# Attention feeding a top-1 mixture of experts on one core: pooled values as 128 and 16 tokens, zero matmuls ahead of the last steps, another order of the attention step

## The chip, the cores and the metric

The kernel runs on 1 core of one Trainium2 chip. The metric is the device time of an execution in microseconds (us). Before the change it was 737.2 us, the median of three runs (732.1 to 743.44).

## The reference

The input has 8 batches of 8 heads with 576 tokens of 64 values. Each head's output is the sum of two attentions: one over the tokens at a distance under 4, and one over sequences pooled by 4 (144 tokens), whose output is repeated four times. The heads side by side give 4608 tokens of 512 values, which pass through the one of eight experts whose embedding lies nearest.

```python
q_d = q.reshape(B, H, Sd, factor, D).mean(axis=3)
k_d = k.reshape(B, H, Sd, factor, D).mean(axis=3)
v_d = v.reshape(B, H, Sd, factor, D).mean(axis=3)
out_up = np.repeat(sm_attn(q_d, k_d, v_d), factor, axis=2)
...
mask = np.abs(pos[:, None] - pos[None, :]) < factor
scores = np.where(mask, scale * np.matmul(q, k.transpose(0, 1, 3, 2)), -1000000000.0)
...
return (out_up + np.matmul(attn, v)).astype(np.float32)
```

```python
logits = xn @ en.T / tau
expert_idx = np.argmax(logits, axis=1)
...
h = np.maximum(x[mask] @ w1[e], 0.0)
out[mask] = gate_w[mask, None] * (h @ w2[e])
```

## The kernel before

**Attention.** A unit of work is one batch and two heads; there are 32 units. `attention()` runs a loop over `i` from -2 to 32, and each pass is one step of a pipeline that has four units in flight. What a pass does is a list of names in `ORDER` (L44). A name with digits is a call of `op_<name>` with these digits as arguments, and `LEAD` says for which unit: the transposes and pooled sums of q and k (`qkT`, `kc`, `pk`, `pq`, `kdT`, `qd`) for unit i+2, the scores and their softmax (`mask scores mx sub expa scd md expd asum add rec an adn`) and the pooled values (`pv`, `vd`) for i+1, the weighted sums (`wT aT wdT adT vald od val xT`) for i, and turning the result into token rows with its logits (`rowsT lastT xr lgt lastrow ls`) for i-1. Nothing reorders these calls: every engine executes its part of them in the order in which they are written, so the table is the order of each engine's queue.

On TensorE (PE), `qkT` (L372) transposes 96 tokens at a time; `mask` (L417) and `scores` (L425) give the local scores, 36 matmuls of 32 queries by 38 keys; `wT` (L483) transposes the local weights `an` into 70 x 128 pieces; `scd` (L445) gives the pooled scores and `wdT` (L495) transposes the pooled weights `ad` in two pieces along the 144 pooled tokens; `vald` (L508) multiplies these with the pooled values `vd`, in two parts that add up in PSUM; `val` (L521) multiplies `aT` with the windows of v (`vw`); `rowsT` and `lastT` (L532) transpose the sum `xT` into rows, and `lgt` (L558) gives the logits. ScalarE (ACT) evicts most of these (`kc` L379, `aT` L490, `adT` L501) and takes the exponentials. VectorE (DVE) does the maxima, sums and scalings (`an` L472, `ad` in `adn` L477, `md` L450, `rec` L467). GpSimd (POOL) makes the pooled sums: `pq` and `pk` L388, `kdT` L399, `qd` L404 and, of the values, `pv` L408 and `vd` L413. All PSUM results rotate through eight banks.

**Loads.** All loads are issued on SP's queue. The k and q of two units (L339) are issued after the last `qkT` of an odd unit, the windows of v (`load_w`, eight transfers, L356 and L362) after its last `val`, and the pooled values (`load_v`, L347) of unit u+3 after `vd` of unit u. A pooled value load reads 4 consecutive tokens into one partition: 72 partitions, twice, with both heads and 256 values.

**What else is in a step.** `Y0` and `Y1` are places at which `attention()` yields to the caller, which may put a slot of expert work there. In the middle of attention that is the first expert's weights: squares (L832) and the splitting of a weight into two half-precision parts, by ACT (L856) and DVE (L857). Near the end, at the pairs in `EARLY`, it is the preparation of the first token lists: `parts` on DVE (L654, L658), 30 small matmuls (L666), `ids` (L670 to L673), and the gathers of rows (L1110). `mid` and `tail` run pieces of `place()`, which once in four units stores a batch's rows (`xd`), finds each token's expert and counts them (L610, L612). `warm_up(n)` issues n matmuls of 128x512 whose result nobody reads.

**Experts.** From about 287 us on, 41 groups of 128 tokens go through two layers of matmuls with split weights (L1213 to L1251).

Of the kernel before, what the change touches and what calls it, by code (L numbers as in the profile page):

```python
# [8 lines left out]
F32 = mybir.dt.float32  # L9
# [10 lines left out]
B, H, S, D = 8, 8, 576, 64  # L20
N, DM, E, FF = B * S, H * D, 8, 1024
NHP = H // 2
SD = S // 4
G, QB = S // 64, 32
WK, WV = QB + 6, 64 + 6
CD = SD // 2
CP = S // 6
TB = 128
NTB = -(-S // TB)
# [12 lines left out]
FIRST = 3  # L42
EARLY = ((8, 1), (9, 1), (10, 1), (11, 1), (27, 0), (27, 1), (28, 0), (29, 0), (29, 1), (30, 0), (30, 1), (31, 0), (31, 1), (32, 1))
ORDER = """  # L44
qkT11 qkT01 qkT10 qkT00 kc11 kc10 mask scores kc01 mx wT1 pq wT0 sub qd1 kc00 mid scd md Y0 qd0 wdT1 pk
wdT0 aT1 aT0 tail share wT2 adT1 kdT pv0 adT0 pv1 expa lastT expd0 lgt asum vald expd2 rowsT expd1 aT2
lastrow od val0 ls add rec Y1 val1 vd an0 an1 xr xT0 xT1 adn
""".split()
FIRST_ORDER = """
mask scores qkT00 qkT01 qkT10 qkT11 kc00 kc10 kc01 kc11 mx sub expa pk pq kdT qd0 qd1 scd md expd0 expd1  # L50
# [12 lines left out]
class Kern:  # L63
# [128 lines left out]
    def attention(self, ctx):  # L192

        nc = self.nc
# [3 lines left out]
        z = self.pool(ctx, "zeroed", 1)  # L198
        self.kq, self.an, self.qdbd, self.vw, self.xT, self.sums = [], [], [], [], [], []
        for i in range(2):  # L200
            self.kq.append(z.tile([128, 2, S + 6], F32, name=f"kq{i}"))
            self.qdbd.append(z.tile([128, 3, 2, 48], F32, name=f"qdbd{i}"))
            self.xT.append(z.tile([128, NTB * TB], F32, name=f"xT{i}"))
            self.an.append(z.tile([128, G, WV], F32, name=f"an{i}"))
            self.sums.append(z.tile([128, G + 3], F32, name=f"sums{i}"))
            self.vw.append(z.tile([WV, G, 4, D], F32, name=f"vw{i}"))
        self.lg = z.tile([TB, NTB, E + 1], F32, name="lg")
        self.oh = self.cp.tile([TB, B, NTB + 1, E], BF16, name="oh")
        units = [(b, hp) for b in range(B) for hp in range(NHP)]
        n = len(units)  # L210
        st, half = {}, {}

        def load(j):
            if j < n // 2:
                half[j] = self.load(j // 2, j % 2)

        pair = {}

        def load_v(u):
            if u < n:  # L220
                pair[u] = self.load_v(*units[u])

        def load_w(j):
            if j < n // 2:
# [9 lines left out]
        for i in range(2):  # L234
            nc.vector.memset(self.kq[i][:, :, :3], 0.0)
            nc.vector.memset(self.kq[i][:, :, S + 3:], 0.0)
            nc.vector.memset(self.vw[i][:32, 0], 0.0)
            nc.vector.memset(self.vw[i][64:, G - 1], 0.0)
            for h in range(2):
                nc.vector.memset(self.qdbd[i][h * D:(h + 1) * D, :, 1 - h], 0.0)  # L240
                nc.vector.memset(self.an[i][h * 64:(h + 1) * 64, :, QB * (1 - h) + 6 * (1 - h):][:, :, :QB], 0.0)
            nc.vector.memset(self.xT[i][:, S:], 0.0)
            nc.vector.memset(self.sums[i], 1.0)
        next(crows)
        load(1)
        load_v(0)
        load_w(0)
        load_v(1)
        lead = {name: k for k, names in LEAD.items() for name in names.split()}

        def table(order):
            ops = []
            for op in order:
                name = op.rstrip("012")
                ops.append((name, [int(x) for x in op[len(name):]]))
            return ops, {name: j for j, (name, _) in enumerate(ops)}

        tail, mid, xr = [], [], {}
        for i in range(-2, n + 1):
            if i == n - 2:  # L260
                self.warm_up(2)
            ops, final = table(FIRST_ORDER if i < NFIRST else ORDER)
            weights = max(final["wT"], final["wdT"])
            for j, (name, args) in enumerate(ops):
# [10 lines left out]
                else:  # L275
                    u = i + lead[name]
# [5 lines left out]
                    s = st[u]  # L282
# [31 lines left out]
            if i >= 1 and units[i - 1][1] == NHP - 1:  # L314
                for f in tail:
                    f()
                b = units[i - 1][0]
                tail = self.place(b, xr[b]["xr"], xr[b]["ls"], mid)
# [20 lines left out]
                    nc.sync.dma_start(out=s[nm][:, :, c], in_=src[b, 4 * hf + c].rearrange("(p m) d -> p m d", m=6))  # L339
        return s  # L340

    def load_v(self, b, hp):
        nc, ld = self.nc, self.ld
        h = slice(2 * hp, 2 * hp + 2)
        vr = ld.tile([CD, 2, 2, 4 * D], F32, name="ld_v", bufs=3)
        for c in range(2):
            nc.sync.dma_start(out=vr[:, c], in_=self.v[b, h, c * S // 2:(c + 1) * S // 2].rearrange(  # L347
                "h (i r) d -> i h (r d)", r=4))
        return vr

    def load_w(self, b, hf, vw):
# [52 lines left out]
        s["g"].tensor_tensor(out=self.qdbd[s["u"] % 2][hs, :, h, :], in0=q2[:, :, :, 0], in1=q2[:, :, :, 1], op=ALU.add)  # L404

    def op_pv(self, s, c, v):
        s["v"], vr = v, v[:, c]
        self.nc.gpsimd.tensor_tensor(out=vr[:, :, 0:2 * D], in0=vr[:, :, 0:2 * D], in1=vr[:, :, 2 * D:], op=ALU.add)  # L408

    def op_vd(self, s):  # L410
        v, vd = s["v"], self.wk.tile([CD, 2, 2, D], F32, name="vd")
        s["vd"] = vd
        self.nc.gpsimd.tensor_tensor(out=vd, in0=v[:, :, :, 0:D], in1=v[:, :, :, D:2 * D], op=ALU.add)  # L413

# [75 lines left out]
        self.nc.scalar.activation(out=dst, in_=s["wT", c], func=AF.Copy)  # L490

    def op_wdT(self, s, c):
        pt = s["wdT", c] = self.bank()[:CD, :288].rearrange("p (c q) -> p c q", c=3)
        for cc in range(3):
            self.nc.tensor.transpose(out=pt[:, cc], in_=s["ad"][:, cc, c * CD:(c + 1) * CD],  # L495
                                     identity=self.ident[:96, :96])

    def op_adT(self, s, c):
        if "adT" not in s:
            s["adT"] = self.wk.tile([CD, 2, 2, 3, 48], F32, name="adT", bufs=1)  # L500
        self.nc.scalar.activation(out=s["adT"][:, c].rearrange("p h c j -> p c h j"),  # L501
                                  in_=s["wdT", c].rearrange("p c (h j) -> p c h j", h=2), func=AF.Copy)

    def op_vald(self, s):
        pd = s["vald"] = self.shared[:, TB:TB + SD]
        for c in range(2):
            for h in range(2):
                self.nc.tensor.matmul(out=pd[h * D:(h + 1) * D], lhsT=s["vd"][:, c, h, :],  # L508
                                      rhs=s["adT"][:, c, h].rearrange("p c j -> p (c j)"),
                                      start=(c == 0), stop=(c == 1))  # L510

    def op_od(self, s):
# [884 lines left out]
```

## Time and profile before

| | before |
|---|---|
| runs | 732.1, 737.2, 743.44 us |
| the profiled execution | 739.52 us, span 737.7 us, mean granted clock 0.972 |
| PE busy | 705.5 us (96%) |
| DVE, ACT, POOL busy | 470.4, 464.9, 444.0 us |
| moved by the core's own queue of loads (q1) | 118.15 MB, 74.8% of 16 engines |

The span is what the trace covers; the profiled execution's own time is 1.8 us longer. "Busy" counts the time in which an engine has an instruction running; PE's ends are modelled, so a busy PE need not be one at its peak. A matmul in the timeline is given as out<-in by the program's names, then the stationary tile (rows*columns) and the moving tile. In brackets stands the idle time ahead of an instruction and what ended it.

### The profile page before, as it was taken

How to read it: one execution, taken by the hardware profiler on the slowest of the kernel's cores; microseconds unless marked ns; L12 is line 12 of the kernel's file. 1: busy time of each engine (PE TensorE's matmuls, PEld its weight loads, DVE VectorE, ACT ScalarE, POOL GpSimd, SP SyncE). 2: the span in 40 equal slices, each digit the busy share in tenths (PEclk: the TensorE clock that was granted, in tenths of full speed). 3: DMA queues.
4: the chain of work that ended last, by engine and by line, in shares of the span. 5: the costliest groups of instructions: out<-in, count | busy, mean ns of one | idle time of the engine just before them, and what ended most of it. 6: DMA issues, size and time to landing. Idle time of an engine off the chain costs nothing. (4 is left out here: it accounts for less than half of the span.)

```text
span 737.7 us, 22025 instructions
## 1 busy us (share of the span) xinstructions
PE 705.5 (96%) x7463; PEld 422.3 (57%) x7463; DVE 470.4 (64%) x1415; ACT 464.9 (63%) x1063; POOL 444.0 (60%) x854
## 2 busy tenths in 40 slices
PE   8999999999999989999999999999999999999992
PEld 5787787878778765454444444444444444444440
DVE  6778789868998775686646566565553455366320
ACT  4777778678787563556666577675665556557420
POOL 4865778766868875366656564646556655664420
PEclk9999899999999887999999999999999999999996
DMA  9899899999888974869988979988997599769830
GB/s 159 168 215 191 209 195 227 215 200 212 164 203 177 207 234 115 194 146 235 218 171 220 241 200 192 225 241 201 225 213 166 116 223 222 151 176 204 168 74 19
DMA packets 283861, 138.92 MB, mean 188 GB/s; under 512 B 250930, under 2 KB 260146, under 8 KB 283712
## 3 DMA queue, kind: packets, MB, share of 16 engines
q1 hardware_dynamic: 276992, 118.15, 74.8%
q0 software_dynamic: 6560, 19.03, 8.1%
q8 instruction: 61, 1.00, 0.6%
q14 instruction: 88, 0.72, 0.3%
q10 hardware_dynamic: 160, 0.02, 0.0%
HBM read 213.05 MB, written 20.33 MB: 316 GB/s over the span
## 5 line engine op out<-in xcount | busy, mean ns | idle before, releaser
L1249 PE MATMUL bank<-w2h,hT 128*128 128x512 f16 x328 | 124.3, 379 | 0.9 <-ACTq L994 0.9
L1214 PE MATMUL bank<-w1l,xT 128*128 128x512 f16 x328 | 124.5, 380 | 0.1
L1215 PE MATMUL bank<-w1h,xT 128*128 128x512 f16 x328 | 124.5, 380 | 0.0
L1213 PE MATMUL bank<-w1h,xT 128*128 128x512 f16 x328 | 124.4, 379 | 0.0
L1251 PE MATMUL bank<-w2h,hT 128*128 128x512 f16 x328 | 124.3, 379 | 0.0
L1250 PE MATMUL bank<-w2l,hT 128*128 128x512 f16 x328 | 124.3, 379 | 0.0
L1110 POOL DMA_INDIRECT xg<-xd,ids x41 | 46.0, 1121 | 79.4 <-POOLq L994 33.6
L1226 ACT ACTIVATE h<-bank 128x512 f16<-128x512 f32 x82 | 48.3, 589 | 56.5 <-PE bank L1215 51.0
L1262 POOL DMA_INDIRECT out_dram<-o,ids x41 | 46.6, 1136 | 47.3 <-ACTq L994 16.6
L379 ACT ACTIVATE kq<-bank 128x288 f32<-128x288 f32 x128 | 48.9, 473 | 34.6 <-PE bank L372 33.5
L832 ACT ACTIVATE junk<-st 128x1024 bf16<-128x1024 f32 (+1 forms) x30 | 67.5, 2251 | 4.1 <-DMA xd<-xr 2.1
L1258 ACT ACTIVATE o<-bank,gt 128x512 f32<-128x512 f32 x41 | 27.8, 677 | 62.0 <-issue 16.3
L408 POOL TENSOR_TENSOR ld_v<-ld_v 72x256 f32<-72x256 f32 x64 | 50.2, 801 | 21.3 <-DMA ld_v<-in_v_dram 20.2
L388 POOL TENSOR_TENSOR pool_kq<-kq 128x288 f32<-128x288 f32 x62 | 44.9, 725 | 30.0 <-ACT kq L379 30.0
L81 POOL TENSOR_SCALAR nw_t<-nw_y,nw_a 128x1 f32<-128x1 f32 x123 | 53.1, 432 | 12.4
L1230 DVE SCALAR_TENSOR_TENSOR h<-bank,h 128x512 f16<-128x512 f32 x82 | 56.3, 687 | 2.7 <-ACTq L1003 2.2
L857 DVE SCALAR_TENSOR_TENSOR w2l<-st,wscl,w2h 128x1024 f16<-128x1024 f32 x32 | 39.6, 1281 | 28.2 <-ACT w2h L856 28.2
L490 ACT ACTIVATE aT<-bank 70x384 f32<-70x384 f32 x96 | 43.9, 490 | 20.7 <-PE bank L483 20.6
L1213 PEld LDWEIGHTS <-xT 128*128 128x128 f16 x328 | 35.2, 107 | 34.0
L1250 PEld LDWEIGHTS <-hT 128*128 128x128 f16 x328 | 32.1, 98 | 39.4 <-issue 1.2
L1215 PEld LDWEIGHTS <-xT 128*128 128x128 f16 x328 | 32.0, 98 | 39.2 <-issue 0.7
L1251 PEld LDWEIGHTS <-hT 128*128 128x128 f16 x328 | 32.1, 98 | 38.7
(220 smaller groups left out, 1559.2 us busy)
## 6 DMA issues: line engine op xcount, KB each, us to landing
st<-in_moe_w_dram SPq DMA_DIRECT2D x148, 1024.0 KB
ld_k<-in_k_dram SPq DMA_DIRECT2D x64, 144.0 KB
ld_q<-in_q_dram SPq DMA_DIRECT2D x64, 144.0 KB
ld_v<-in_v_dram SPq DMA_DIRECT2D x64, 144.0 KB
xd<-xr SPq DMA_DIRECT2D x8, 1040.0 KB
st<-in_moe_w_dram SPq DMA_DIRECT2D x16, 512.0 KB
vw<-in_v_dram SPq DMA_DIRECT2D x64, 122.5 KB
vw<-in_v_dram SPq DMA_DIRECT2D x32, 64.0 KB
```

What stands on the lines that cost most here:

```text
L81: g.tensor_scalar(out=t, in0=y, scalar1=y, scalar2=a, op0=ALU.mult, op1=ALU.mult)
L379: self.nc.scalar.activation(out=dst, in_=s["qk", r, w].rearrange("p (m i) -> p i m", m=3), func=AF.Copy, scale=(KSC, QSC)[w])
L408: self.nc.gpsimd.tensor_tensor(out=vr[:, :, 0:2 * D], in0=vr[:, :, 0:2 * D], in1=vr[:, :, 2 * D:], op=ALU.add)
L832: self.nc.scalar.activation(out=junk, in_=src, func=AF.Square, accum_out=acc)
L1213: nc.tensor.matmul(out=ps, lhsT=xT[:, 0, k], rhs=self.w1h[:, k, ns], start=(k == 0), stop=False)
L1214: nc.tensor.matmul(out=ps, lhsT=xT[:, 0, k], rhs=self.w1l[:, k, ns], start=False, stop=False)
L1215: nc.tensor.matmul(out=ps, lhsT=xT[:, 1, k], rhs=self.w1h[:, k, ns], start=False, stop=(k == self.KC - 1))
L1226: self.nc.scalar.activation(out=h2[:, 0], in_=ps, func=AF.Relu)
L1230: self.nc.vector.scalar_tensor_tensor(out=h2[:, 1], in0=ps, scalar=0.0, in1=h2[:, 0], op0=ALU.max, op1=ALU.subtract)
L1249: nc.tensor.matmul(out=ps, lhsT=hh, rhs=self.w2h[:, j, :], start=(j == 0), stop=False)
L1250: nc.tensor.matmul(out=ps, lhsT=hh, rhs=self.w2l[:, j, :], start=False, stop=False)
L1251: nc.tensor.matmul(out=ps, lhsT=hl, rhs=self.w2h[:, j, :], start=False, stop=(j == self.FC - 1))
```

## The change

Three parts. `CD`, the number of pooled tokens in each of the two pieces, goes from 72 and 72 to 128 and 16; with it the pooled value loads, `pv`, `wdT`, `adT` and the two parts of `vald` have 128 and 16 rows (or columns). The tiles for the loads are no longer taken from a rotating pool but are three fixed ones, whose second halves POOL sets to zero once at the start, since `vd` adds all 128 partitions of both halves. `warm_up` is called ahead of the last three passes (2, 2 and 6 matmuls) instead of once (2). And `ORDER` is another table.

```diff
-CD = SD // 2
+CD = (128, SD - 128)
...
 ORDER = """
-qkT11 qkT01 qkT10 qkT00 kc11 kc10 mask scores kc01 mx wT1 pq wT0 sub qd1 kc00 mid scd md Y0 qd0 wdT1 pk
...
+qkT10 qkT01 qkT00 mask qkT11 kc01 kc00 kc11 scores mx wT2 kc10 aT2 sub wT1 wT0 aT1 pq qd0 scd aT0 wdT1 qd1
...
+        self.vr = [z.tile([128, 2, 2, 4 * D], F32, name=f"ld_v{i}") for i in range(3)]
...
-                pair[u] = self.load_v(*units[u])
+                pair[u] = self.load_v(*units[u], self.vr[u % 3])
...
+        for vr in self.vr:
+            nc.gpsimd.memset(vr[:, 1], 0.0)
...
-            if i == n - 2:
-                self.warm_up(2)
+            if i >= n - 2:
+                self.warm_up((2, 2, 6)[i - n + 2])
...
-    def load_v(self, b, hp):
-        nc, ld = self.nc, self.ld
-        h = slice(2 * hp, 2 * hp + 2)
-        vr = ld.tile([CD, 2, 2, 4 * D], F32, name="ld_v", bufs=3)
-        for c in range(2):
-            nc.sync.dma_start(out=vr[:, c], in_=self.v[b, h, c * S // 2:(c + 1) * S // 2].rearrange(
-                "h (i r) d -> i h (r d)", r=4))
+    def load_v(self, b, hp, vr):
+        h, t0 = slice(2 * hp, 2 * hp + 2), 0
+        for c, n in enumerate(CD):
+            self.nc.sync.dma_start(out=vr[:n, c], in_=self.v[b, h, t0:t0 + 4 * n].rearrange("h (i r) d -> i h (r d)", r=4))
+            t0 += 4 * n
         return vr
...
-        s["v"], vr = v, v[:, c]
+        s["v"], vr = v, v[:CD[c], c]
...
-        v, vd = s["v"], self.wk.tile([CD, 2, 2, D], F32, name="vd")
+        v, vd = s["v"], self.wk.tile([128, 2, 2, D], F32, name="vd")
...
-        pt = s["wdT", c] = self.bank()[:CD, :288].rearrange("p (c q) -> p c q", c=3)
+        pt = s["wdT", c] = self.bank()[:CD[c], :288].rearrange("p (c q) -> p c q", c=3)
         for cc in range(3):
-            self.nc.tensor.transpose(out=pt[:, cc], in_=s["ad"][:, cc, c * CD:(c + 1) * CD],
+            self.nc.tensor.transpose(out=pt[:, cc], in_=s["ad"][:, cc, c * CD[0]:c * CD[0] + CD[c]],
                                      identity=self.ident[:96, :96])
...
-                self.nc.tensor.matmul(out=pd[h * D:(h + 1) * D], lhsT=s["vd"][:, c, h, :],
-                                      rhs=s["adT"][:, c, h].rearrange("p c j -> p (c j)"),
+                self.nc.tensor.matmul(out=pd[h * D:(h + 1) * D], lhsT=s["vd"][:CD[c], c, h, :],
+                                      rhs=s["adT"][:CD[c], c, h].rearrange("p c j -> p (c j)"),
                                       start=(c == 0), stop=(c == 1))
```

What the new table moves, engine by engine. The queue of PE over the second half of a steady step, from the local scores to the weighted sums, before (the names are those of the tiles, the sizes rows and columns of the operands as the program writes them):

```order
L425 MATMUL bank<-kq_109 32x38 x36
L483 MATMUL bank<-ident,an_106 70x128 x6
L445 MATMUL bank<-kdT,qdbd_110 96x144 x3
L495 MATMUL bank<-ident,ad 72x96 x6
L483 MATMUL bank<-ident,an_106 70x128 x3
L532 MATMUL bank<-ident,xT_111 128x128
L558 MATMUL bank<-xT_111,enT 32x192 x4
L508 MATMUL bank<-adT,vd 64x144 x4
L532 MATMUL bank<-ident,xT_111 128x128 x4
L521 MATMUL bank<-aT,vw_114 64x64 x18
```

and with the change:

```order
L426 MATMUL bank<-kq_109 32x38 x36
L484 MATMUL bank<-ident,an_106 70x128 x9
L446 MATMUL bank<-kdT,qdbd_110 96x144 x3
L496 MATMUL bank<-ident,ad 16x96 x3
L496 MATMUL bank<-ident,ad 128x96 x3
L533 MATMUL bank<-ident,xT_111 128x128 x4
L559 MATMUL bank<-xT_111,enT 32x192 x4
L533 MATMUL bank<-ident,xT_111 128x128
L509 MATMUL bank<-adT,vd 64x144 x4
L522 MATMUL bank<-aT,vw_108 64x64 x18
```

All nine transposes of `an` now stand ahead of the pooled scores, the pooled weights are transposed as 16 and 128, and four of the five row transposes stand ahead of the logits and of `vald`. Ahead of these rows, `mask` has moved between the third and the fourth of the `qkT`.

The queue of DVE in a step in which a weight is split (L857, with the change L858), before:

```order
L472 TENSOR_TENSOR an_112<-a,sums_113 64x9x38 x2
L526 TENSOR_TENSOR xT_105<-bank,od 128x320
L526 TENSOR_TENSOR xT_105<-bank,od 128x256
L477 TENSOR_TENSOR ad<-ad,sums_113 96x432
L432 TENSOR_REDUCE mx<-bank 128x9
L436 TENSOR_TENSOR a<-bank,mx 128x342
L450 TENSOR_REDUCE md<-bank 96x3
L857 SCALAR_TENSOR_TENSOR w2l<-st_483,wscl,w2h 128x1024
```

and with the change:

```order
L473 TENSOR_TENSOR an_106<-a,sums_107 64x9x38 x2
L527 TENSOR_TENSOR xT_111<-bank,od 128x256
L527 TENSOR_TENSOR xT_111<-bank,od 128x320
L858 SCALAR_TENSOR_TENSOR w2l<-st_557,wscl,w2h 128x1024
L478 TENSOR_TENSOR ad<-ad,sums_107 96x432
L433 TENSOR_REDUCE mx<-bank 128x9
L437 TENSOR_TENSOR a<-bank,mx 128x342
L451 TENSOR_REDUCE md<-bank 96x3
```

The split, work of `Y0`, has moved from behind `md` to between `xT` and the scaling of `ad`. The `parts` of the token lists now come at `Y1`, between `rec` and `an`, and their matmuls (L666) at the `Y0` behind `val`.

SP's queue of loads, over two steps, before:

```order
L356 DMA vw_114<-in_v_dram 64x4x64
L356 DMA vw_114<-in_v_dram 3x4x64
L362 DMA vw_114<-in_v_dram 70x7x64 x4
L356 DMA vw_114<-in_v_dram 64x4x64
L356 DMA vw_114<-in_v_dram 3x4x64
L347 DMA ld_v<-in_v_dram 72x2x256 x4
L339 DMA ld_k<-in_k_dram 96x6x64 x2
L339 DMA ld_q<-in_q_dram 96x6x64 x2
```

and with the change:

```order
L348 DMA ld_v_115<-in_v_dram 128x2x256
L348 DMA ld_v_115<-in_v_dram 16x2x256
L357 DMA vw_108<-in_v_dram 64x4x64
L357 DMA vw_108<-in_v_dram 3x4x64
L363 DMA vw_108<-in_v_dram 70x7x64 x4
L357 DMA vw_108<-in_v_dram 64x4x64
L357 DMA vw_108<-in_v_dram 3x4x64
L348 DMA ld_v_116<-in_v_dram 128x2x256
L348 DMA ld_v_116<-in_v_dram 16x2x256
L342 DMA ld_k<-in_k_dram 96x6x64 x2
L342 DMA ld_q<-in_q_dram 96x6x64 x2
```

The pooled loads of two units stood together between the windows and k and q; now one stands on either side of the windows.

More of the change, by code (lines that the diff above doesn't have):

```diff
@@ L44 @@
 ORDER = """
-qkT11 qkT01 qkT10 qkT00 kc11 kc10 mask scores kc01 mx wT1 pq wT0 sub qd1 kc00 mid scd md Y0 qd0 wdT1 pk
-wdT0 aT1 aT0 tail share wT2 adT1 kdT pv0 adT0 pv1 expa lastT expd0 lgt asum vald expd2 rowsT expd1 aT2
-lastrow od val0 ls add rec Y1 val1 vd an0 an1 xr xT0 xT1 adn
+qkT10 qkT01 qkT00 mask qkT11 kc01 kc00 kc11 scores mx wT2 kc10 aT2 sub wT1 wT0 aT1 pq qd0 scd aT0 wdT1 qd1
+adT1 md wdT0 pk adT0 kdT pv1 expa mid expd1 share tail rowsT expd2 lgt asum lastT vald expd0 od lastrow xr
+ls pv0 val1 vd add rec Y1 val0 an1 an0 xT1 xT0 Y0 adn
 """.split()
@@ L499, in op_adT @@
         if "adT" not in s:
-            s["adT"] = self.wk.tile([CD, 2, 2, 3, 48], F32, name="adT", bufs=1)
-        self.nc.scalar.activation(out=s["adT"][:, c].rearrange("p h c j -> p c h j"),
+            s["adT"] = self.wk.tile([128, 2, 2, 3, 48], F32, name="adT", bufs=1)
+        self.nc.scalar.activation(out=s["adT"][:CD[c], c].rearrange("p h c j -> p c h j"),
                                   in_=s["wdT", c].rearrange("p c (h j) -> p c h j", h=2), func=AF.Copy)
```

## The prediction

> **What bounds the kernel now.** I first cut the span into stretches (columns: length, then busy time and count of PE, PEld, DVE, ACT, POOL, then the granted TensorE clock, the DMA share and GB/s).
>
> ```profile
> 40.00:160.00 120.00, 114.45 (x2384) 94.23 (x2382) 95.26 (x245) 91.81 (x287) 84.89 (x133) 0.96 0.97 209
> 160.00:250.00 90.00, 89.04 (x1865) 73.19 (x1865) 80.38 (x201) 70.44 (x228) 68.26 (x106) 1.00 0.87 193
> 250.00:287.00 37.00, 32.57 (x479) 24.20 (x478) 21.84 (x71) 18.53 (x56) 27.19 (x55) 0.72 0.65 170
> 287.00:737.70 450.70, 433.87 (x2131) 203.05 (x2128) 244.91 (x815) 259.81 (x420) 237.12 (x505) 0.99 0.80 185
> ```
>
> The last 450 us are expert matmuls at a full clock; the change doesn't reach them. In attention PE is the busiest engine everywhere, and between 40 and 160 the DMA engines are full as well. One attention step has one mask matmul, so the distance of these gives the step (count, durations, first and last start):
>
> ```profile
> L417 PE MATMUL bank<-mask,identb x15: 308/310/493, 39.9 to 158.1; 128*128 128x342 bf16 x15
> L417 PE MATMUL bank<-mask,identb x11: 310/310/310, 166.7 to 244.7; 128*128 128x342 bf16 x11
> ```
>
> 14 steps in 118.2 us are 8.44 each; 10 steps in 78.0 are 7.80. How short a step can be, I read from the timeline of PE over a step in which PE never waits:
>
> ```profile
> 212.64 0.71 PE L372 MATMUL bank<-ident,ld_q 96*128 96x96 f32 x6
> ...
> 216.12 0.66 PE L495 MATMUL bank<-ident,ad 96*72 96x96 f32 x6
> 216.62 0.49 PE L483 MATMUL bank<-ident,an 128*70 128x128 f32 x3
> 216.95 0.27 PE L532 MATMUL bank<-ident,xT 128*128 128x128 f32 x1
> 217.15 0.53 PE L558 MATMUL bank<-xT,enT 128*32 128x192 f32 x8
> 217.61 0.71 PE L508 MATMUL bank<-adT,vd 72*64 72x144 f32 x8
> 218.25 0.66 PE L532 MATMUL bank<-ident,xT 128*128 128x128 f32 x4
> 218.84 1.27 PE L521 MATMUL bank<-aT,vw 70*64 70x64 f32 x36
> 220.04 0.71 PE L372 MATMUL bank<-ident,ld_q 96*128 96x96 f32 x6
> ```
>
> From 212.64 to 220.04 are 7.40 us. What lies between that and the real steps is in the table of waits and in the clock:
>
> ```profile
> PEld bank L521 <- DMA vw<-in_v_dram: 3.3, 7, 0.9
> PE bank L521 <- DMA vw<-in_v_dram: 2.3, 6, 0.8
> PE bank L483 <- DVE an L472: 1.1, 2, 0.6
> PE bank L495 <- DVE ad L477: 0.3, 1, 0.3
> ```
>
> ```profile
> 84.93:88.34 3.41, 2.55 (x44) 1.91 (x42) 2.19 (x7) 2.17 (x10) 3.32 (x6) 1.00 0.59 129
> 88.34:95.17 6.83, 6.74 (x100) 5.57 (x101) 3.87 (x9) 2.76 (x6) 5.40 (x10) 0.50 0.91 206
> 156.60:160.02 3.42, 3.42 (x87) 2.88 (x85) 0.98 (x4) 2.79 (x6) 2.96 (x4) 0.50 0.88 197
> 248.76:252.18 3.42, 3.22 (x74) 2.63 (x72) 2.38 (x11) 2.17 (x10) 2.38 (x5) 1.00 0.68 177
> 252.18:262.42 10.24, 8.50 (x103) 6.77 (x104) 4.62 (x11) 2.76 (x6) 8.52 (x10) 0.50 0.97 197
> 272.66:276.07 3.41, 1.74 (x42) 1.63 (x42) 2.75 (x12) 2.91 (x8) 2.59 (x9) 1.00 0.06 25
> 276.07:286.31 10.24, 9.96 (x88) 6.27 (x85) 5.21 (x19) 3.92 (x9) 7.08 (x16) 0.50 0.27 53
> ```
>
> PE's waits for the local value windows (vw) come to some 5.6 us, nearly all between 40 and 160. Four stretches ran at half clock, each after a window of 3.41 us in which the array did less than usual (only windows around a loss are shown). At half clock half the time is lost: 5.1 us in the two stretches before 161, and 5.1 in each of the two behind 250 if PE works through them.
>
> So there are two regimes: to 160 loads and their aftermath cost about 10.9 us (118.2 less 14 x 7.66, where 7.66 is 7.80 less the 0.14 a step that PE waited for an and ad); behind 160 PE's own stream is the step.
>
> **The change, part by part.** *(a) Order of the stream on PE.* In the timeline the transposes of 128 columns start every 0.11 us (three from 216.62 to 216.95). After the single one of L532 the next matmul starts 0.20 later, so 0.09 is lost where the stationary tile goes from 128*128 to 128*32. The four of L532 take 0.59 to the start of L521 instead of 0.44: 0.15 lost, going to 70*64. I therefore price a change between tiles that round up to different sizes (32, 64 or 128 rows or columns) at 0.09 to 0.15, and at nothing where only the true size differs (96*96 to 128*70). The step before has seven such changes. The new one has ten: into scores and out of them, into and out of wdT1, whose tile is now 96*16, into lgt and out of it again to lastT, into the first half of vald (128*64), into its second half (16*64), into val, and out of val. Three more are 0.27 to 0.45 a step; I take 0.40, because most changes go to or from a 64-row or 32-row tile like the 0.15 one. The transposes read 96 x 3 columns either way and vald 144 x 4, so the uneven split saves no streaming. Below nothing isn't excluded (fewer waits for evictions), but PE doesn't wait for those now. The dense step becomes 7.80 (7.67 to 7.85).
>
> *(b) Loads of 128 and 16 rows.* The page gives the size, and a quiet window after the last two pooled loads the packets (packets, MB, share):
>
> ```profile
> ld_v<-in_v_dram SPq DMA_DIRECT2D x64, 144.0 KB
> ```
>
> ```profile
> q1 hardware_dynamic: 327, 0.30, 32.1%
> ```
>
> Two loads of 72 x 2 rows of 1 KB are 288 packets, a small piece of vw 12, and 27 remain. As one completion for each engine taking part this reads 12, 12 and 3: a 72-row load fills 12 of 16 engines. If 128 and 16 rows fill all 16, four loads in two steps put 36 KB instead of 48 on the busiest engines. At 209 GB/s over 16 engines, 13 KB a us, that is 0.9 us in 16.9, 5%. The Trainium skill, page "DMA: Bandwidth & Descriptors", section "Why a DMA increments its semaphore by 16 and not by 1", says that a transfer goes on the largest number of engines up to 16 that divides its outer sizes: 12 for 72, 16 for 128 and 16. The packets agree; by the page the 36 KB are sure.
>
> With 5% less to fetch in a step that PE's changes make 5% longer, the loads come early enough in most steps. Both ends: all 10.9 us go, or none (the same bytes, and vw still shares the queue). SP now issues one pooled load behind each step's vd, so that the vw of a pair stands behind k/q and two more issues, where it stood behind k/q alone; that keeps me from the upper end. I take three quarters: 10.9 falls to 2.7. Steps 40 to 160: 14 x (7.66 + 0.40) + 2.7 = 115.5 against 118.2, **-2.7**. The four steps ahead of 40, at 0.40 each: **+1.6**.
>
> *(c) Vector order.* Between 160 and 250, twelve steps x 0.40: **+4.8**. The weight splits move from behind md to just ahead of ad's scaling:
>
> ```profile
> 214.88 0.83 DVE L477 TENSOR_TENSOR ad<-ad,sums 96x432 f32<-96x432 f32 x1
> ...
> 217.12 1.27 DVE L857 SCALAR_TENSOR_TENSOR w2l<-st,wscl,w2h 128x1024 f16<-128x1024 f32 x1
> ```
>
> Queued behind the split are ad, then mx, sub and md; wdT on PE waits for ad. Here ad was done at 215.71, 0.41 ahead of wdT (216.12); the third wT, now ahead of wdT, adds 0.33 and a tile change 0.1, so its slack is about 0.85 and the split's 1.27 exceeds it by 0.4 to 0.5. For the eight splits within attention the cost is 0 to 4; I take 0.25 each, +2.0. The 1.4 us of waits for an and ad in the old order (rows above) go, as the split no longer stands ahead of an: together **+0.6**.
>
> *(d) POOL.* Pooled sums over 128 and 16 rows instead of 72 and 72 cost nothing if time goes with the free size alone:
>
> ```profile
> L404 POOL TENSOR_TENSOR qdbd<-pool_kq 64x144 f32<-64x144 f32 x58 | 28.4, 490 | 4.4
> L399 POOL TENSOR_TENSOR kdT<-pool_kq 128x144 f32<-128x144 f32 x29 | 15.0, 518 | 1.8
> L686 POOL MEMSET xg<- 128x520 f32 x4 | 2.1, 532 | 0.2
> ```
>
> 64 and 128 rows differ by 28 ns. The three new memsets are 0.53 each by the last row, 1.6 together, and lie in POOL's first wait:
>
> ```profile
> 13.15 1.29 POOL L388 TENSOR_TENSOR pool_kq<-kq 128x288 f32<-128x288 f32 x2 [6.48 <-ACT kq L379]
> ```
>
> 6.48 us of idle time cover them; uncovered they would cost 1.6.
>
> *(e) The last steps.* Two more steps x 0.40, **+0.8**. The 30 small matmuls of L666 now stand closer behind the vector work that makes their operand:
>
> ```profile
> 247.89 0.78 DVE L654 TENSOR_TENSOR eq<-sfirst,pb 128x90 f32<-128x90 f32 x1
> 248.70 0.61 DVE L658 TENSOR_TENSOR parts<-eq,thi 128x90 bf16<-128x90 f32 x1
> ...
> 250.58 0.91 PE L666 MATMUL bank<-parts,at 128*128 128x6 bf16 x30
> ```
>
> Before, the first parts were done 1.3 us ahead of L666. Now these vector operations (1.6 us with a third of 0.25) follow rec, and L666 follows val at once; PE comes there at about the time of rec, so I take 1.3 of the 1.6 as a wait (0 to 1.9 with an ahead in the queue): **+1.3**, and the stretch at half clock behind 252 stays. The zeros go ahead of the last two steps and the last, two and six of them. Six hold PE 1.3 us at the pace of the expert part, where 6 x 328 matmuls of this size take the 433.87 us of the first table, 0.22 each; they lie in this wait:
>
> ```profile
> 275.59 1.02 PE L483 MATMUL bank<-ident,an 128*70 128x128 f32 x6 [1.67 <-DVE an L472]
> ```
>
> Two of them put 0.43 us of full-array work into the window from 272.66, which had 1.74; that window would then resemble 84.93 (2.55) less than the ordinary ones, so avoiding the loss behind it isn't sure: 0 to -5.1, I take **-3.0**.
>
> Sum: -2.7 + 1.6 + 4.8 + 0.6 + 0.8 + 1.3 - 3.0 = +3.4 on the profiled execution's 739.5, or 742.9. That execution was 2.3 over the median of 737.2; so 740.6, and I say **740**: no difference that can be told. Its own range is 731 to 749.
>
> **The rivals.** *Loads were the bound (0.20).* All 10.9 us between 40 and 160 go, the stretch behind 252 (fetch waits stand ahead of it) keeps its clock, -5.1, as does 276, -3.0; a tile change costs 0.09, 31 steps x 0.27 = +8.4; waits for an go, -1.4. 739.5 - 12.0 - 2.3 = 725. For it speaks the DMA share of 0.97; against it 0.87 behind 160, where steps are no longer than PE's stream.
>
> *The new order costs more than it frees (0.13).* Tile changes cost 0.15, 31 x 0.45 = +14.0; ad is late by 0.5 in eight steps, +4.0; L666 waits, +1.3; the loads' waits and all half clocks stay. 739.5 + 19.3 - 2.3 = 756. It decides once the steps from 160 to 250 pass 8.3 us. For it: PE has no slack there (89.0 busy of 90). Against: full stays of the loads' waits in a longer step.
>
> *The zeros do nothing (0.21).* The clock behind 276 halves as before: 740.6 + 3.0 = 744. For it: 3.22 us busy from 248.76 didn't keep the clock either. The Trainium skill, "TensorE: Matmul & The Clock Gate", section "Part 1: The HAM clock gate (the "warmup" mystery)", has the clock fall only after an idle window of about 3.4 us; by that rule zeros between work bring nothing, this rival's time. The trace disagrees with the rule: no window ahead of a loss was idle.
>
> **How the numbers follow.** The forecast has 0.46. Two per cent, 14.7 us, is about what a measurement of this kernel can tell from no change: below 722.5 is faster, above 752 slower. Faster: not quite half of the first rival and a little of the forecast, 0.13. Slower: two thirds of the second and a little of the rest, 0.11. Same: 0.76. The range reaches to the first rival's far side and the second's near one: 722 to 755.
>
> **What would show it.** Right: dense steps of 7.7 to 7.85 with pauses around 96*16 and 16*64; steps of 8.2 to 8.3 between 40 and 160 and of 8.2 between 160 and 250; the DMA share there below 0.95; full clock behind 276. Wrong: steps to 160 still at 8.4 or more (loads not relieved), or steps behind 160 at 7.8 (tile changes are hidden), or waits of wdT for ad in most steps; a gain over 10 us would say that loads bounded far more than the waits show.

## The result, and the profile after

The changed kernel takes 741.34 us (median of 20 runs, 735.91 to 748.84) against 736.55 for the kernel before in as many runs: a ratio of 1.0055, with a 95% interval of 1.0033 to 1.0076. The interval excludes 1, so the kernel is slower, by 0.6%, well under the prediction's bound of 2%. The forecast was 740, from a sum of +3.4 us.

The profiled execution took 744.87 us with a span of 743.1, 5.4 more than before. The distance between landmarks says where that lies (the k-th mask matmul, counted from 0, in the two timelines):

| stretch | before | after | difference |
|---|---|---|---|
| start to mask 4 | 39.93 | 40.91 | +1.0 |
| masks 4 to 18, 14 steps | 118.1 | 116.8 | -1.4 |
| masks 18 to 28, 10 steps | 78.8 | 85.6 | +6.8 |
| masks 28 to 31, 3 steps | 30.0 | 26.8 | -3.2 |
| mask 31 to PE's last matmul | 456.8 | 457.2 | +0.4 |
| from there to the end | 14.1 | 15.9 | +1.8 |

A stretch of one execution is not exact to a microsecond. The experiment without the added zeros (below) is the same program up to the last steps, and its execution has 120.8 and 82.6 us where the changed kernel has 116.8 and 85.6. The last row is steadier: all six profiled kernels with the new layout and the new table need 15.6 to 16.1 us from PE's last matmul to the end, the other eight 13.9 to 14.4. The prediction has no term for it; its cause stays open.

First the same stretches of the span as before, with the same columns:

```profile
40.00:160.00 120.00, 114.22 (x2411) 93.97 (x2406) 98.49 (x248) 93.05 (x287) 89.54 (x141) 0.99 0.90 207
160.00:250.00 90.00, 84.72 (x1725) 69.34 (x1724) 73.18 (x185) 68.61 (x215) 66.66 (x99) 0.98 0.87 197
250.00:287.00 37.00, 33.39 (x607) 25.66 (x603) 27.18 (x86) 22.63 (x70) 29.87 (x56) 0.91 0.49 147
```

The DMA share between 40 and 160 fell from 0.97 to 0.90 while the GB/s stayed (209 and 207): the same bytes occupy the DMA engines for less time. Between 160 and 250 PE went from 89.0 busy of 90 to 84.7: there it now waits. The clock between 250 and 287 rose from 0.72 to 0.91.

The dense step, from the timeline of PE in the changed kernel:

```profile
217.99 0.47 PE L373 MATMUL bank<-ident,ld_k 96*128 96x96 f32 x3
...
221.81 0.66 PE L496 MATMUL bank<-ident,ad 96*16 96x96 f32 x6
222.31 0.60 PE L533 MATMUL bank<-ident,xT 128*128 128x128 f32 x4
222.84 0.53 PE L559 MATMUL bank<-xT,enT 128*32 128x192 f32 x8
223.30 0.33 PE L533 MATMUL bank<-ident,xT 128*128 128x128 f32 x1
223.56 0.86 PE L509 MATMUL bank<-adT,vd 128*64 128x144 f32 x8
224.35 1.27 PE L522 MATMUL bank<-aT,vw 70*64 70x64 f32 x36
225.55 0.47 PE L373 MATMUL bank<-ident,ld_k 96*128 96x96 f32 x3
```

It is 225.55 - 217.99 = 7.56, so 0.16 more than before and not 0.40. Start to start, wdT took 0.50 before (216.12 to 216.62) and takes 0.50 now, though three of its six tiles are 96*16; the five row transposes take 0.79 in both; vald went from 0.64 to 0.79. So 0.15 of the 0.16 lies in vald, whose second part now has a 16*64 tile behind a 128*64 one. (The first row of a group names the group: "96*16 x6" are three of 96*16 and three of 96*128.)

And the waits of PE in the changed kernel, up to 260:

```profile
PE bank L496 <- DVE ad L478: 3.9, 5, 1.2
...
PE bank L426 <- issue: 3.3, 3, 2.1
...
PE bank L484 <- issue: 2.0, 1, 2.0
...
PE bank L667 <- DVE parts L659: 1.5, 1, 1.5
```

The waits for vw are off this list. The prediction put them at 5.6 us before, but that sum counts most pauses twice, once on PE and once on its weight loads (PEld), as one of them shows:

```profile
88.42 0.30 PEld L521 LDWEIGHTS bank<-aT,vw 70*64 70x64 f32 x4 [0.93 <-DMA vw<-in_v_dram]
88.43 0.48 PE L521 MATMUL bank<-aT,vw 70*64 70x64 f32 x4 [0.79 <-DMA vw<-in_v_dram]
```

On PE alone they were 2.3 us between 20 and 252, and up to 300:

```profile
PE bank L521 <- DMA vw<-in_v_dram: 2.8, 7, 0.8
```

In their place stand waits for ad (3.9 us, in five steps, 0.37 to 1.25 each), the wait of the list matmuls for parts, 1.5 against a forecast of 1.3, and two stalls of 2.0 and 2.1 us inside groups of PE that wait for nothing the profile shows. Between masks 4 and 18, PE was idle for 5.6 us before and is for 5.8 now; what fell there is the time at half clock, from 8.3 us to 3.4.

### The profile page after: what moved, and what is told of

It reads as the page before. It is cut to its first block, busy times and chain, and to the rows that moved or that the text cites. A ratio compares the mean times of both kernels' runs of the same rounds, so it can differ in the third digit from the quotient of the medians.

```text
span 743.1 us, 22102 instructions
## 1 busy us (share of the span) xinstructions
PE 704.9 (95%) x7471; PEld 419.8 (56%) x7471; DVE 472.5 (64%) x1415; ACT 469.0 (63%) x1063; POOL 453.1 (61%) x857
## 5 line engine op out<-in xcount | busy, mean ns | idle before, releaser
L389 POOL TENSOR_TENSOR pool_kq<-kq 128x288 f32<-128x288 f32 x62 | 55.3, 893 | 48.8 <-ACT kq L380 42.1
L380 ACT ACTIVATE kq<-bank 128x288 f32<-128x288 f32 x128 | 50.6, 476 | 19.3 <-PE bank L373 17.1
L858 DVE SCALAR_TENSOR_TENSOR w2l<-st,wscl,w2h 128x1024 f16<-128x1024 f32 x32 | 39.5, 1279 | 26.1 <-ACT w2h L857 24.2
L491 ACT ACTIVATE aT<-bank 70x384 f32<-70x384 f32 x96 | 40.1, 482 | 23.6 <-PE bank L484 23.4
L1251 PEld LDWEIGHTS <-hT 128*128 128x128 f16 x328 | 32.0, 98 | 39.4 <-issue 1.2
L1252 PEld LDWEIGHTS <-hT 128*128 128x128 f16 x328 | 32.0, 98 | 38.8
L1250 PEld LDWEIGHTS <-hT 128*128 128x128 f16 x328 | 32.0, 98 | 38.7 <-DMA hT<-h 0.3
```

The lines of the kernel that those rows point to most:

```text
L380: self.nc.scalar.activation(out=dst, in_=s["qk", r, w].rearrange("p (m i) -> p i m", m=3), func=AF.Copy, scale=(KSC, QSC)[w])
L389: s["g"].tensor_tensor(out=s["t2"][:, w], in0=k4[:, :, 0:2], in1=k4[:, :, 2:4], op=ALU.add)
L1250: nc.tensor.matmul(out=ps, lhsT=hh, rhs=self.w2h[:, j, :], start=(j == 0), stop=False)
L1251: nc.tensor.matmul(out=ps, lhsT=hh, rhs=self.w2l[:, j, :], start=False, stop=False)
L1252: nc.tensor.matmul(out=ps, lhsT=hl, rhs=self.w2h[:, j, :], start=False, stop=(j == self.FC - 1))
```

## The experiments

Each was timed against the kernel before on the same chip. Ratios are to the kernel before, with 95% intervals. The theory after the result: the layout relieves the loads and costs 0.15 us a step; the new table costs more than the prediction had, chiefly where the splits stand ahead of ad.

**The layout alone.** The changed kernel with the table and the zeros of before:

```diff
-qkT10 qkT01 qkT00 mask qkT11 kc01 ...
+qkT11 qkT01 qkT10 qkT00 kc11 kc10 mask scores ...
-            if i >= n - 2:
-                self.warm_up((2, 2, 6)[i - n + 2])
+            if i == n - 2:
+                self.warm_up(2)
```

> The kernel before with the 128/16 layout alone (old order, old zeros). My theory: the second part of vald on 16 rows costs one tile change of 0.15 us in each of 31 steps (dense step 7.55 instead of 7.40), +4.7; the loads on 16 engines end the waits for vw between 40 and 160 (5.6 us in the profile of before, under 1.5 here) and with them a half-clock stretch, -4 to -9: ratio 0.993 to 1.001. Rival (the layout doesn't relieve the loads, the order does): dense step 7.55 and vw still waited for 4 us or more, ratio 1.004 to 1.008.

Measured: 0.9940 (0.9912 to 0.9969). The dense step is 7.55. The waits of PE:

```profile
PE bank L484 <- DVE an L473: 3.6, 6, 1.4
PE bank L496 <- DVE ad L478: 1.1, 3, 0.5
...
PE bank L522 <- DMA vw<-in_v_dram: 0.4, 2, 0.2
```

PE's waits for vw are down from 2.8 to 0.4 us in this profile. They don't stay there: the kernel with zeros and layout in the old table (below), the same program up to the last steps, has 3.0. The queue of the loads between 40 and 160, first before and then here (packets, MB, share of 16 engines):

```profile
q1 hardware_dynamic: 61120, 24.76, 96.2%
```

```profile
q1 hardware_dynamic: 61779, 24.70, 89.6%
```

As many bytes with 6.6 points less of the engines' time (90.1% in the kernel with zeros); the prediction had put it at 5%. The layout gains 4.4 us although it pays 31 x 0.15 = 4.7 on PE. So the theory holds for the time and the dense step. That it works through the waits for vw isn't shown; what both profiles of this layout have less of is time at half clock, 13.7 and 6.8 us between 20 and 300 against 30.7 before. Over all executions the difference is smaller: a mean granted clock of 0.979 and 0.981 against 0.976.

**The table alone**, in the kernel before (72 and 72, one pair of zeros):

```diff
-qkT11 qkT01 qkT10 qkT00 kc11 kc10 mask scores ...
+qkT10 qkT01 qkT00 mask qkT11 kc01 ...
```

> The kernel before with the new ORDER alone (72/72, old zeros). My theory: dense step 7.40; wdT waits for ad by 0.4 to 1.3 us in six or more of the eight steps with a split, +4 to +6; loads on 12 engines keep most of the waits for vw: ratio 1.003 to 1.010. Rival (the order relieves the loads): waits for vw under 1.5 us, ratio 0.994 to 1.001.

Measured: 1.0137 (1.0093 to 1.0181), some 10 us, more than either theory had.

```profile
PE bank L521 <- DMA vw<-in_v_dram: 6.0, 5, 1.8
PE bank L425 <- issue: 3.6, 3, 1.4
PE bank L495 <- DVE ad L477: 3.6, 6, 1.1
PE bank L666 <- DVE parts L658: 1.8, 1, 1.8
```

In this profile the new order doesn't relieve the loads, and it adds waits for ad and parts, and the stalls called issue. So the layout (0.994) and the table (1.0137) pull apart, and their product, 1.0076, is near the 1.0055 of the whole change, which has the zeros too.

**128 rows in both parts of vald**, in the changed kernel. The second parts of vd and of adT hold zeros beyond 16 rows, so that the sums stay what they are:

```diff
+        nc.gpsimd.memset(self.adT[:, 1], 0.0)
...
-                self.nc.tensor.matmul(out=pd[h * D:(h + 1) * D], lhsT=s["vd"][:CD[c], c, h, :],
-                                      rhs=s["adT"][:CD[c], c, h].rearrange("p c j -> p (c j)"),
+                self.nc.tensor.matmul(out=pd[h * D:(h + 1) * D], lhsT=s["vd"][:, c, h, :],
+                                      rhs=s["adT"][:, c, h].rearrange("p c j -> p (c j)"),
```

> The changed kernel with the second part of vald over all 128 rows (112 of them zeros in both operands), which leaves the arithmetic as it is and takes the tile change between the parts away. My theory: dense step 7.40 to 7.42 instead of 7.56, some 4.5 us less than the changed kernel, ratio 0.998 to 1.001. Rival (PE's stream doesn't set the step, or the rows of the tile aren't what costs): dense step unchanged or no shorter time, ratio 1.004 to 1.007.

Measured: 1.0059 (1.0028 to 1.0090), no gain over the changed kernel that can be told, though the shortest steady steps are down to 7.26 to 7.41.

```profile
PE bank L523 <- DMA vw<-in_v_dram: 5.0, 7, 1.7
PE bank L498 <- DVE ad L480: 4.4, 5, 1.5
```

The waits for vw are 5.0 us, more than in any profile with the new table and 16 rows (none in two, 1.3 to 3.5 in three). That PE waits for the loads what it saves in a step fits this, but waits that differ so much from one execution to the next don't prove it.

**The same in the old order** (layout, 128 rows, table and zeros of before; the diff is that of the layout alone and of the 128 rows):

> The kernel before with the 128/16 layout and the second part of vald over 128 rows (zeros in both operands), old order, old zeros. Theory 1 (PE's stream sets the step, 0.15 us a step are to be had): dense step 7.40, 3 to 5 us less than the layout alone at 0.994, ratio 0.987 to 0.990. Theory 2 (with a shorter step the loads bound again, as with 128 rows in the new order): waits for vw of 3 us or more come back, ratio 0.992 to 0.996.

Measured: 0.9914 (0.9886 to 0.9942). From one step of its timeline:

```profile
218.75 0.71 PE L510 MATMUL bank<-adT,vd 128*64 128x144 f32 x8
219.40 0.66 PE L534 MATMUL bank<-ident,xT 128*128 128x128 f32 x4
```

vald takes 0.65 again and the dense step (213.78 to 221.18) 7.40. This is the fastest kernel tried and faster than both, but against the layout alone the gain, 0.26%, lies within the intervals. Its 3.0 us of waits for vw are what the kernel with zeros, layout and 16 rows has too, so they can't be put down to the 128 rows. The dense step is as theory 1 has it; the time lies between the two theories' ranges.

**Y0 back behind md**, in the changed kernel:

```diff
-adT1 md wdT0 pk adT0 ... xT1 xT0 Y0 adn
+adT1 md Y0 wdT0 pk adT0 ... xT1 xT0 adn
```

> The changed kernel with Y0 back behind md, so that the splits no longer stand ahead of ad. My theory: the waits of wdT for ad in the split steps (0.37 to 1.25 us, six of eight in the profile of the changed kernel) go to under 0.5 us in all, 4 to 5 us less than the changed kernel, ratio to before 0.998 to 1.001. Rival (the split only moves the wait, as it then stands ahead of an): waits for an take their place, ratio within 0.003 of the changed kernel's 1.0055.

Measured: 1.0069 (1.0037 to 1.0100): nothing gained. No wait of PE for ad is left, but:

```profile
PE bank L509 <- ACT adT L502: 6.3, 13, 1.7
PE bank L484 <- DVE an L473: 3.2, 6, 0.8
```

In this table wdT0 and adT0 follow md, so ACT's squares and splits of Y0 now stand ahead of adT0, which vald waits for. The rival was right in kind, though the next wait is another than it named.

**adn ahead of Y0**, in the changed kernel:

```diff
-ls pv0 val1 vd add rec Y1 val0 an1 an0 xT1 xT0 Y0 adn
+ls pv0 val1 vd add rec Y1 val0 an1 an0 xT1 xT0 adn Y0
```

> The changed kernel with adn ahead of Y0 at the step's end, so that only the split's place against ad changes. Theory: ad was late in PE's queue; its waits (4 to 5 us in the changed kernel) go to under 0.5 us and nothing takes their place, as mx behind the split has PE's scores to wait for anyway: ratio to before 0.998 to 1.001. Rival (as with Y0 behind md, the time goes to the next wait: mx, adT, or loads that are not there yet): ratio 1.004 or more, and 3 us or more of other waits that the changed kernel doesn't have.

Measured: 1.0042 (1.0015 to 1.0069).

```profile
PE bank L522 <- DMA vw<-in_v_dram: 3.5, 6, 0.9
PE bank L446 <- POOL at L631: 2.1, 1, 2.1
```

The waits for ad are gone, and this profile has waits for vw in their place and a longer one for POOL's list work (2.1 us against 1.1 in the changed kernel); a gain over the changed kernel can't be told. That splits ahead of ad are the main price of the table, my theory, falls.

**Without the added zeros**, the changed kernel otherwise:

```diff
-            if i >= n - 2:
-                self.warm_up((2, 2, 6)[i - n + 2])
+            if i == n - 2:
+                self.warm_up(2)
```

> The changed kernel with the zeros of before (two, once). Theory of the prediction: without them the clock behind 277 stays at half for longer than one window (10.2 us in the kernel before, 3.4 with the zeros), +3: ratio 1.007 to 1.011. Rival (the zeros do nothing for the clock and cost at most their own 1.7 us): ratio 1.002 to 1.006.

Measured: 1.0096 (1.0062 to 1.0130), 0.4% or 3.0 us above the changed kernel; the intervals still overlap a little. Its last step on PE:

```profile
285.77 1.27 PE L522 MATMUL bank<-aT,vw 70*64 70x64 f32 x36
288.69 0.66 PE L533 MATMUL bank<-ident,xT 128*128 128x128 f32 x4 [1.65 <-DVE xT L527]
...
290.69 0.61 PE L1214 MATMUL bank<-w1h,xT 128*128 128x512 f16 x1 [0.62 <-DMA xT<-x]
291.09 0.63 PE L1215 MATMUL bank<-w1l,xT 128*128 128x512 f16 x1
```

The wait for xT that the six zeros would fill stays empty, and the first expert matmuls take 0.63 us instead of 0.38 and start every 0.43 instead of 0.22: half the clock. From mask 31 to PE's last matmul it is 459.4 us; in the table alone, also without the zeros, 459.6; with the new table and the zeros 455.1 to 457.2 in five profiles. The clock agrees: in the 40 us behind mask 31, the two profiles with the new table and without the zeros lost two windows of 3.4 us to half clock, of the five with both four lost none and the changed kernel one.

**Zeros and layout, old table.**

```diff
-qkT10 qkT01 qkT00 mask qkT11 kc01 ...
+qkT11 qkT01 qkT10 qkT00 kc11 kc10 mask scores ...
```

> The changed kernel with the table of before: layout and zeros, old order. Theory: the zeros only mend a wait that the new table makes at the end (first expert matmuls 459.5 us ahead of PE's last one in the two profiles with the new table and without zeros, 455 to 457 with them, 455 to 457 with the old table without them), so they bring nothing here: ratio 0.993 to 0.997, as the layout alone. Rival (zeros bring 3 us under any table): 0.988 to 0.991.

Measured: 0.9957 (0.9925 to 0.9989), the same as the layout alone within the intervals. The times show no gain from the zeros under the old table. That there is nothing to mend under it is not so for the clock: behind mask 31 the kernel before ran 10.2 us at half clock and the layout alone 3.4, this one none. One wait of 2.8 us for kdT, which the layout alone doesn't have, takes the place. And the waits for vw:

```profile
PE bank L522 <- DMA vw<-in_v_dram: 3.0, 5, 1.0
```

**Only Y0 moved.** The kernel just above, with one name of its table moved to where the new table has it:

```diff
-wT0 sub qd1 kc00 mid scd md Y0 qd0 wdT1 pk ... an0 an1 xr xT0 xT1 adn
+wT0 sub qd1 kc00 mid scd md qd0 wdT1 pk ... an0 an1 xr xT0 xT1 Y0 adn
```

> As e9_old_order_zeros, with Y0 moved from behind md to just ahead of adn, as the new table has it, and nothing else of the new table. Theory: Y0's place is the dearest part of the new table (splits ahead of ad, the token lists' parts late for their matmuls): wdT waits for ad 3 to 5 us, the list matmuls for parts 1.5, ratio 0.999 to 1.004. Rival (the price lies elsewhere in the table): within 0.002 of e9_old_order_zeros.

Measured: 1.0113 (1.0070 to 1.0155), 1.6% above the kernel without the move, with the intervals far apart. In the old table this one place costs as much as the whole new table does. It doesn't explain the new table by itself: there, putting Y0 back behind md brought nothing (1.0069), as ACT's share of it then stood ahead of adT0.

```profile
PE bank L496 <- DVE ad L478: 5.9, 8, 1.5
PE bank L426 <- issue: 3.9, 3, 2.6
PE bank L373 <- DMA ld_q<-in_q_dram: 2.1, 1, 2.1
PE bank L667 <- DVE parts L659: 1.8, 1, 1.8
```

**Y0 behind adn**, one step more of the same:

```diff
-... xT0 xT1 Y0 adn
+... xT0 xT1 adn Y0
```

> As e10_y0_late (old table, layout, zeros, Y0 at the step's end, 1.0113), but with Y0 behind adn instead of ahead of it: the only thing moved is DVE's scaling of ad against the work of Y0. Theory: ad late (5.9 us of waits in eight steps, a half-clock stretch of 10 us behind one of them) is most of the 1.6% that the place costs: waits for ad under 1 us, ratio 0.996 to 1.002. Rival (the rest of Y0 is what costs at that place: its loads ahead of k and q on SP, ACT's squares and splits, the list matmuls): ratio 1.006 or more.

Measured: 1.0075 (1.0036 to 1.0113). Waits for ad are down to 0.6 us, but the kernel stays clearly above the 0.9957 with Y0 behind md:

```profile
PE bank L522 <- ACT aT L491: 2.0, 5, 0.5
PE bank L373 <- DMA ld_q<-in_q_dram: 1.7, 2, 0.9
PE bank L522 <- DMA vw<-in_v_dram: 1.7, 6, 0.4
```

So the lateness of ad isn't the whole price. By the ratios it is 0.4 of the 1.6%, and the rest of Y0 at that place the larger part, but the intervals of this kernel and the last one overlap. What the traces show of it: Y0 now follows Y1 almost at once. In the kernel before, the pieces of the first expert's weights, 512 KB each, were issued 7 us and more apart; with Y0 late, four of the eight come in two pairs. SP's queue, before and with Y0 late (ahead of adn):

```profile
44.49 0.63 SPq L876 DMA_DIRECT2D st<-in_moe_w_dram  x1
51.74 0.39 SPq L876 DMA_DIRECT2D st<-in_moe_w_dram  x1
62.30 0.63 SPq L876 DMA_DIRECT2D st<-in_moe_w_dram  x1
```

```profile
53.63 0.41 SPq L877 DMA_DIRECT2D st<-in_moe_w_dram  x1
55.11 0.42 SPq L877 DMA_DIRECT2D st<-in_moe_w_dram  x1
70.60 0.41 SPq L877 DMA_DIRECT2D st<-in_moe_w_dram  x1
```

Two pieces 1.5 us apart stand right ahead of the next k and q, and by the table ACT's squares and splits of the two yields fall together ahead of aT. That this crowding is the cause is argued from the waits above; it wasn't tried by itself.

**SP's sequence.** vd ahead of the last val, which gives SP the new table's sequence of loads in the old table:

```diff
-lastrow od val0 ls add rec Y1 val1 vd an0 an1 xr xT0 xT1 adn
+lastrow od val0 ls add rec Y1 vd val1 an0 an1 xr xT0 xT1 adn
```

> As e9_old_order_zeros, with vd ahead of the last val, which gives SP's queue the sequence of the new table (a pooled load on either side of the windows) and nothing else of it. Theory: the windows vw then come later; waits for vw of 3 us or more (0.4 with the layout alone), ratio 0.998 to 1.003. Rival (the sequence of the loads doesn't matter): within 0.002 of e9_old_order_zeros.

Measured: 0.9950 (0.9918 to 0.9982), the same as without it. In the old table the sequence of the loads, for which the prediction held back a part of the gain, doesn't show in the time; in the new one it wasn't tried.

**Stores in pieces.** The changed kernel, with the rows of the first five batches stored in four pieces over four steps:

```diff
-            save(nc.sync)
+            save(0, 1 if spread else NTB)
...
+            if spread:
+                save(1, 2)
```

> The changed kernel with the rows of the first five batches stored in four pieces over four steps instead of 1040 KB at once. Theory: the stalls of 1.1 to 2.3 us in the middle of PE's own groups, with nothing waited for, 5 us behind a store (184.7 and 212.0 in the changed kernel) come from instruction fetches that queue behind the store's packets; without the burst none over 1 us is left within 160 and 250, ratio 0.998 to 1.003. Rival (the stalls don't hang on the stores): stalls over 1 us at such places as before, ratio 1.004 to 1.008.

Measured: 1.0133 (1.0099 to 1.0168), slower than the changed kernel. The edit brought a wait of its own: around 103 ACT idles 5.4 us until the last piece is stored, because the buffer of rows is used again:

```profile
103.51 0.28 ACT L554 ACTIVATE xr<-bank 128x128 f32<-128x128 f32 x1 [5.40 <-DMA xd<-xr]
```

As for the stalls it aimed at, none of 1 us called issue is left between 160 and 250, but one profile and another wait in it settle nothing about their cause.

## Why the forecast came out right, and which of its terms were wrong

The time, its smallness and its sign came out as forecast, and of the rivals' times none did; the nearest, that the zeros do nothing, was 744. But that is in good part luck: the sum hit because two terms were wrong by about 8 us each, on opposite sides. Of the prediction's own signs, the DMA share of 0.90 and the steps of 8.3 us between masks 4 and 18 came. The dense step of 7.56 lies below its 7.67 to 7.85, the steps between masks 18 and 28 took 8.6 instead of 8.2, past the 8.3 at which it would have sided with its second rival, and half clock came back behind 276.

**(a) Tile changes: mis-sized.** Three more a step at 0.40 were forecast, +12.8 over the 32 steps of the sum; measured 0.16, or +5.1. The step that failed is the pricing by size alone: the pairs into and out of the 96*16 tile of wdT, a transpose, cost nothing, and the reordered row transposes took as long as before. The one change that costs, 128*64 to 16*64 in vald, costs the 0.15 read from L532. The Trainium skill, page "TensorEngine Tiling (Array Packing)", section "Key Properties", says that a change of tiling mode drains TensorE. The 0.15 would fit that, though no trace names the mode, and the transposes show no such cost here.

**(b) Loads: right in size and direction, not in place.** Forecast: 5% less DMA, and three quarters of the 10.9 us lost up to 160, 8.2. The share of the loads' queue fell by 6.6 points, and the layout alone gave 4.4 us net of its 4.7 on PE, so 9 gross. But the 10.9 us were not what the prediction took them for. Its 5.6 us of waits for vw were 2.3 on PE; the rest of PE's idle time there had other causes (a stall of 0.9, adT, aT and an at 0.6 each). And the gain doesn't lie where it was priced. Up to the same step (masks 4 to 18; the layout with zeros is the kernel in the old table):

| masks 4 to 18, us | before | changed | layout alone | layout with zeros |
|---|---|---|---|---|
| length | 118.1 | 116.8 | 115.5 | 115.3 |
| PE idle | 5.6 | 5.8 | 3.3 | 4.0 |
| of it, waiting for vw | 2.3 | 0 | 0.4 | 3.0 |
| at half clock | 8.3 | 3.4 | 4.5 | 2.8 |

The two kernels with the old table gain 2.7 and 2.9 us here, or 4.8 and 5.0 with the 14 x 0.15 that they pay, and another 4.8 and 6.2 between masks 28 and 31 (25.2 and 23.8 us against 30.0), where the kernel before ran at half clock from 252.18 to 262.42. Whether relieved loads keep the clock up there is not shown. The changed kernel's -1.4 instead of -2.7, though PE's stream grew less than forecast, is due to waits for ad and lists and to a stall, which fill the place of the waits for vw.

**(c) The table: sign right, far too small.** This is the step that failed on the other side. Forecast +0.6 for the splits ahead of ad and +1.3 for parts, besides (a). The table alone, which has none of the tile changes in vald, cost 1.4%, 10 us. Waits for ad measured 3.2 to 5.9 in the kernels that have them, instead of 2.0; the second rival's figure was 4.0; and in the old table Y0 at the step's end cost 1.6% by itself, by the ratios most of it not through ad. The prediction followed one DVE instruction of Y0 through the queues, and not its loads, ACT's work and the distance to Y1; that these are the cause is argued, not tried one by one. Between masks 18 and 28, +6.8 against +5.4 came from other things than forecast: 10 x 0.16 and 4.3 us more idle time on PE, which is 5.3 us in all, 3.1 in two stalls and 2.2 for ad.

**(d) POOL: right for what it priced.** mask 0 came no later with the memsets (0.9 us earlier), and PE has no wait for pv or vd among the four above. One wait of 1.1 us at 127 for kdT, behind POOL's list work, wasn't in the forecast.

**(e) The end: right in its terms, with one term missing.** From mask 28 to PE's last matmul the changed kernel gained 2.8 against a forecast of 0.9. But the last 450 us, which the change was said not to reach, took 1.8 more behind that matmul, so that -1.0 is left in all. The wait for parts came (1.5). The zeros brought 3.0 us by the timing, the forecast's number, though the intervals overlap a little, and they act through the clock: half clock came back behind 280 for one window of 3.4 us instead of three before. Of nine profiles with the added zeros, eight had no half clock in the 40 us behind mask 31; of five without, one. By the Trainium skill's rule of the idle window ("TensorE: Matmul & The Clock Gate", section "Part 1: The HAM clock gate (the "warmup" mystery)", named in the prediction) they would have brought nothing; these clocks speak against that.

**The start** cost 1.0 of the forecast 1.6, but not by tile changes: masks 0 to 1 took 10.4 us instead of 8.2, at half clock. It isn't the layout either: with zeros and layout in the old table they took 8.2 again.

## What to carry to other kernels

When loads and one engine are both near their bound, time the parts of a change apart: here a layout that gave 0.6% and an order that took 1.4% looked together like a change that does nothing. A place at which other work may enter (Y0) is a bundle; follow its loads, every engine's share and its distance to the next such place before pricing it by one instruction. A sum of waits over PE and PEld counts pauses twice; and a wait is gone only when a second profile of the same steps says so too: the waits for vw were 0.4 us in one and 3.0 in another. A step shortened on PE needn't shorten the kernel: of 0.15 us a step, nothing showed in the new table and 0.26% in the old, within the intervals.

## What the runs showed of the hardware that was not expected

**Tiles.** Within one group of matmuls, going from 128 rows to 16 rows cost 0.15 us (0.64 to 0.79); padding to 128 rows with zeros took it away (0.65). Transposes by 96*16 tiles between 96*128 ones cost nothing measurable (0.50 for six in both).

**PE stalls that wait for nothing.** In the changed kernel PE stopped in the middle of its scores (start, duration, group; in brackets the idle time ahead):

```profile
181.92 0.65 PE L426 MATMUL bank<-kq 64*32 64x38 f32 x48
184.68 0.41 PE L426 MATMUL bank<-kq 64*32 64x38 f32 x24 [2.12 <-issue]
185.02 2.14 PE L484 MATMUL bank<-ident,an 128*70 128x128 f32 x9
```

The last row shows what followed: the clock stood at half from 185.0 to 188.4, and the nine transposes, 1.18 us in other steps, took 2.14. The stall that ends at 75.7 was followed by half clock from 75.7 to 79.2 in the same way. Two such windows are 3.4 us lost, on top of the 4.1 of the stalls. Not every stall is followed by one: in the kernel without the added zeros, one of 1.97 us that ends at 79.5 is not.

Around the stall one 16 KB packet of an instruction queue lands, and a store had been issued 5.6 us before it began:

```profile
q8 instruction: 1, 0.02, 2.9%
```

```profile
176.92 0.56 SPq L582 DMA_DIRECT2D xd<-xr  x1
```

Between 160 and 250 such stalls of 1 us or more appeared in six of the nine kernels with the new table or a late Y0 (1.1 to 2.6 us, at 181 to 186, 207 to 213 or near 246 to 250), and in none with the old table and Y0 behind md. That instruction fetches wait behind bursts of other transfers would fit; no run here proves it, and spreading the stores didn't settle it.
